# Attention and two expert layers on one core: the first expert prepared in border pools, output sums added in DRAM, scales from sums of squares, the seven products reordered

## Chip, core and metric

One NeuronCore of a Trainium2 chip runs the whole program in one launch. The metric is the time of one execution in microseconds (us), as the device measures it. The engines are PE (TensorE, the matrix unit), DVE (VectorE), ACT (ScalarE), POOL (GpSimd) and SP (SyncE, which issues DMAs); "the clock" is the TensorE clock granted, 1.00 being 2.4 GHz.

## What is computed

Three layers, cut to what matters:

```
x = attention(q, k, v, s)                       # 4 x 8 heads, 576 rows, 64 columns
x = gelu_like(x @ w_in) @ w_out                 # 2304 tokens, 512 -> 2048 -> 512
P = balance(softmax(x @ w_gate))                # 8 rounds over rows and columns
out = sum over e of P[:, e] * (relu(x @ w1[e]) @ w2[e])    # 8 experts, 512 -> 1024 -> 512
```

Every expert sees every token. The change touches the third layer and its beginning, which lies inside the end of the second.

## The kernel before

**Order of the work.** The kernel does not issue its instructions as it goes. Each one is handed to a planner, the class Sequencer, which keeps a time for every engine, gives each instruction a cost (`cost`) and a rank, and decides the order in which instructions go into each engine's queue. PE's steps come from generators that yield until their operands are ready by the planner's clock; held instructions of the other engines follow by readiness, rank and number. The result is a fixed list for each engine, which the chip works through in order: an instruction that waits holds up all behind it on its engine. All instructions carry the line of one helper (L260), so rows are told apart by tile names.

**Second layer's end.** `first_moe` ends with a wide stage: the last two token blocks go through `wide1` and `wide2` together, 16 steps, with dense PE work. Beside it, `begin_second` prepares the first third of the tokens for the experts (`prep_x(0)`), and half way through, when some weight buffers have become free, `begin_weights` prepares the first expert: `prep_w1(0, 0)`, `prep_w1(0, 1)`, then at lower priority `prep_w2(0)` and `prep_x(1)`.

**Third layer.** For each expert e and each third tp of the tokens (768 of them): four calls of `unit1` (j = 0 to 3; hidden columns) and then three calls of `unit2` (i = 0 to 2; output rows). That is 24 such thirds in all. Each unit is a matrix product in a Strassen-Winograd scheme with seven products instead of eight, every operand split into two f16 halves (three matmuls for each product and block of rows). A unit works in four PSUM banks A, B, C and D and chains its seven products through them: B starts as a copy of A, C as a copy of B. Two units are in flight at a time, in two sets of banks; PE takes the older one that is ready. Of `unit1`, a product is 6 matmuls of 384 columns; of `unit2`, 12 of 256.

In `unit1` the order of products is 0, 6, 5, 1, 4, 3, 2. The tile `hst` collects seven f32 pieces of hidden values, of which `parts` makes the f16 halves `h` in three groups of 3, 2 and 2 pieces: ACT writes the high half, DVE the low one. Product 3 goes into bank D on top of product 6, but DVE must first have read D for `hst[1]`, and that instruction also needs `v`, which ACT makes from bank C after product 4.

`unit2` needs the `h` of all four j, and begins with all 12 matmuls of product A(0, 0), then D(3, 6). Its seven products end in `acc2`, 18 tiles of 128 x 512 f32 that stay in SBUF through all experts: `put` adds to them with a DVE instruction each.

**Preparing an expert.** `weight_scales(e)` reads w1 and w2 of one expert (16 tiles `wm`), takes the largest absolute value on DVE and sends it through DRAM (`mx`, `row`) to all partitions. `prep_w1` and `prep_w2` load the weights again (`wr`), make the seven combinations and split them into halves (`w1o`, and `wo`, which goes to DRAM as `w2_d` and comes back as `w2o`). `prep_x` does the same for tokens (`xr`, `xo`, `xc_d` in DRAM, `xt` when loaded). `after1` sets them going: expert e + 1's scales at tp = 0, its w2 at tp = 1, its w1 at tp = 2.

Of the kernel before, what the change touches and what calls it, by code (L numbers as in the profile page):

```python
# [33 lines left out]
W2_ORDER = (0, 6, 5, 1, 4, 3, 2)  # L34
# [16 lines left out]
class Sequencer:  # L51
# [68 lines left out]
    def cost(self, engine, what, out, ins):  # L120
        n = max(self.size(x) for x in [out] + ins[:2])
        psum = any(x.space == PSUM for x in ins)
        if self.fine:
            if engine == "PE":
                return self.size(out) * (4 if ins[0].dtype == F32 else 1) / 2.4 + (13 if ins[0].dtype == F32R else 5)
            if engine == "DVE":
                quick = what in ("tensor_copy", "tensor_scalar") and not psum
                return 150 + n / (1.92 if quick else 0.96)
            if engine == "ACT":
                return 180 + n / 1.2  # L130
# [12 lines left out]


    def submit(self, engine, what, call, outs, ins):
# [5 lines left out]
        if what == "dma_start":  # L151
            op.cost = 60
            op.nbytes = self.size(outs[0]) * outs[0].shape[0] * 4
        else:
            op.cost = self.cost(engine, what, outs[0], ins)
# [146 lines left out]
def kernel(  # L302
# [45 lines left out]
    pa = ExitStack()  # L348
    wpool = Pool(seq, p1.enter_context(tc.tile_pool(name="wpool", bufs=1, side=left, reuse_waits="tile")))
# [783 lines left out]
    def scale_of(key, cols):  # L1133

        i = len(sc_of)
        sm = mem["small"]
# [21 lines left out]
        sc_of[key], inv_of[key] = s2[:, 0:1], s2[:, 1:2]  # L1158

    def raw(shape, name):  # L1160
        return mem["ep"].tile(shape, F32, tag="raw", name=name, bufs=7)

    def largest(col, x):
        nc.vector.tensor_reduce(out=col, in_=x, axis=AX.XY, op=ALU.max, apply_absolute_value=True)

    def weight_scales(e):

        mx = mem["small"].tile([128, 2, 8], F32, tag="wmx", name="wmx", bufs=2)
        for i in range(8):
# [5 lines left out]
            largest(mx[:, 0, i:i + 1], st)  # L1175
        scale_of(("w1", e), mx[:, 0])
        for i in range(8):
            st = raw([128, 1, DM], "wm")
            nc.sync.dma_start(out=st, in_=w2[e, i * 128:(i + 1) * 128, :].rearrange("p (o d) -> p o d", o=1))
            largest(mx[:, 1, i:i + 1], st)  # L1180
        scale_of(("w2", e), mx[:, 1])
# [111 lines left out]
    def prep_w2(e):  # L1293

        sc = sc_of["w2", e]
        for half in range(2):
# [10 lines left out]
            def part(i, src):  # L1307
                o = mem["ep"].tile([128, 2, 2, 256], F16, tag="xo", name="wo", bufs=2)
# [9 lines left out]

    xc_d = [dram.tile([128, 7, 2, 2, HT], F16, name=f"xc_d{tp}") for tp in range(NTP)]
# [62 lines left out]
    def cring(name):  # L1382
        return mem["c"].tile([128, HT], F32, tag="c", name=name, bufs=5)

    def unit1(e, tp, j, s):
# [28 lines left out]
        def parts(k0, k1, relu):  # L1414
            src = st[:, k0:k1]
# [17 lines left out]
        prod(d, 6)  # L1433
        yield ready(5, settled(b))
# [3 lines left out]
        u2, v, r21 = cring("u2"), cring("v"), cring("r21")  # L1438
        out_of(u2, b)
        yield ready(1, settled(a))  # L1440
        prod(a, 1, first=False)
        st = mem["st"].tile([128, 7, HT], F32, tag="hst", name="hst", bufs=2)
        seq.rank = 1
        out_of(st[:, 0], a, ACTF.Relu)
# [13 lines left out]
        if j == 0 and (e or tp):  # L1458
# [5 lines left out]
        parts(0, 3, True)  # L1464
        nc.vector.tensor_tensor(out=st[:, 3], in0=st[:, 0], in1=r21, op=ALU.subtract)
        nc.vector.scalar_tensor_tensor(
            out=st[:, 4], in0=st[:, 1], scalar=0.0, in1=r21, op0=ALU.max, op1=ALU.add
        )
        parts(3, 5, False)
        nc.vector.tensor_tensor(out=st[:, 5], in0=st[:, 4], in1=st[:, 0], op=ALU.subtract)  # L1470
        nc.vector.scalar_tensor_tensor(
            out=st[:, 6], in0=st[:, 2], scalar=0.0, in1=st[:, 5], op0=ALU.max, op1=ALU.subtract
        )
        parts(5, 7, False)
# [4 lines left out]
    def unit2(e, tp, i, s):  # L1479
# [7 lines left out]
        c11, c12 = acc2[t0][:, 0:256], acc2[t0][:, 256:512]  # L1487
        c21, c22 = acc2[t1][:, 0:256], acc2[t1][:, 256:512]
        ts = slice(i * 128, i * 128 + 128)

        def ready(k, n, *more):
            def when():
                t = max(ok(w[:, n]), *[m() for m in more])
                for j in range(NJ):
# [12 lines left out]
        def prod(o, k, n, first=True):  # L1507
            m = 0
            for j in range(NJ):
                for ph, pw in ((0, 0), (0, 1), (1, 0)):  # L1510
                    nc.tensor.matmul(
                        o, lhsT=hs[e, tp, j][:, ph, k, ts], rhs=w[:, n, pw, j],
                        start=(first and m == 0), stop=(m == 3 * NJ - 1), skip_group_check=not first,
                    )
                    m += 1

        def put(out, bank, t, first=True):
            if e == 0 and first:
                nc.scalar.activation(out=out, in_=bank, func=ACTF.Copy, scale=qs[0][:, tp:tp + 1])
            else:  # L1520
                by = pq[e][:, t:t + 1] if e else qs[0][:, tp:tp + 1]
                nc.vector.scalar_tensor_tensor(
                    out=out, in0=bank, scalar=by, in1=out, op0=ALU.mult, op1=ALU.add
                )

        def leave(t):
            if e == E - 1:
                nc.sync.dma_start(out=out[t * 128:(t + 1) * 128, :], in_=acc2[t])

        yield ready(0, 0, free("A"))  # L1530
        if e == 1:
            seq.rank = 1
            for t in (t0, t1):
                nc.vector.tensor_scalar(
                    out=acc2[t], in0=acc2[t], scalar1=prob[:, t, 0:1], scalar2=None, op0=ALU.mult
                )
            seq.rank = 0
        past[s] = False
        a = bank_tile("A", s)[:, 0:256]
        prod(a, 0, 0)  # L1540
        b = bank_tile("B", s)[:, 0:256]
        nc.scalar.copy(out=b, in_=a)
        yield ready(3, 6, free("D"))
        d = bank_tile("D", s)[:, 0:256]
        prod(d, 3, 6)
# [4 lines left out]
        yield ready(2, 1, settled(a))  # L1550
        prod(a, 2, 1, first=False)
        put(c11, a, t0)
        past[s] = True
        yield ready(4, 4, settled(c))
        prod(c, 4, 4, first=False)
        put(c22, c, t1)
        put(c22, d, t1, False)
        yield ready(1, 3, settled(d))
        prod(d, 1, 3, first=False)
        if e:  # L1560
            put(c21, d, t1)
            put(c21, b, t1)
        else:
            put(c21, b, t1)
            put(c21, d, t1, False)
        leave(t1)
        yield ready(6, 2, settled(c))
        prod(c, 6, 2, first=False)
        put(c12, c, t0)
        leave(t0)  # L1570
# [21 lines left out]
    def begin_second():  # L1592
# [4 lines left out]
        ))  # L1597
        mem["ps"] = Pool(seq, ctx.enter_context(
# [16 lines left out]
        )  # L1615
        seq.rank = 0

    def begin_weights():

# [3 lines left out]
        load_x2(0)  # L1623
        prep_w1(0, 0)
        prep_w1(0, 1)
        seq.rank = 3
        prep_w2(0)
        prep_x(1)
# [128 lines left out]
    wide2()  # L1757
    wpool.flush()
# [5 lines left out]
    for i in range(NTILE):  # L1764
        acc2[i] = xpool.tile([128, DM], F32, name=f"acc{i}")
# [99 lines left out]
    def after1(e, tp, j):  # L1865
# [6 lines left out]
        if tp == 0 and e + 1 < E:  # L1872
# [3 lines left out]
        if (e, tp) == (0, NTP - 1):  # L1876
# [113 lines left out]
```

## Time and profile before

| what | us |
|---|---|
| median of 3 runs (2237.88 to 2240.2) | 2238.88 |
| the profiled execution, its own time | 2241.58 |
| its span in the trace | 2239.7 |
| PE busy | 2001.8 (89%) |
| DVE busy | 1529.5 (68%) |
| ACT busy | 1099.3 (49%) |
| POOL busy | 364.1 (16%) |

PE is the engine with the most work, and matmuls overlap, so its busy time is not its least time; how far PE is from dense work is read from the distance between starts of equal groups. "Idle before" in a row is the time that the engine stood still before the group, with the instruction whose end released it.

### The profile page before, as it was taken

How to read it: one execution, taken by the hardware profiler on the slowest of the kernel's cores; microseconds unless marked ns; L12 is line 12 of the kernel's file. 1: busy time of each engine (PE TensorE's matmuls, PEld its weight loads, DVE VectorE, ACT ScalarE, POOL GpSimd, SP SyncE). 2: the span in 40 equal slices, each digit the busy share in tenths (PEclk: the TensorE clock that was granted, in tenths of full speed). 3: DMA queues.
4: the chain of work that ended last, by engine and by line, in shares of the span. 5: the costliest groups of instructions: out<-in, count | busy, mean ns of one | idle time of the engine just before them, and what ended most of it. 6: DMA issues, size and time to landing. Idle time of an engine off the chain costs nothing.

```text
span 2239.7 us, 40229 instructions
## 1 busy us (share of the span) xinstructions
PE 2001.8 (89%) x15782; PEld 1570.5 (70%) x15782; DVE 1529.5 (68%) x3120; ACT 1099.3 (49%) x2018; POOL 364.1 (16%) x376
## 2 busy tenths in 40 slices
PE   5889999999996598579999999999999999999998
PEld 3788999999874465446666666666666667766676
DVE  8886665545356265677786776778678778778555
ACT  6875655445335454444553453454455454345333
POOL 7774453443341210000000000000000000000000
PEclk9999999999998799789999999999999999999999
DMA  7454332221233534632343344335245234334220
GB/s 220 146 175 148 93 96 88 68 67 54 69 122 127 187 117 136 201 111 89 120 154 109 125 162 124 117 124 191 95 134 184 94 100 170 118 125 158 78 78 29
DMA packets 182897, 274.58 MB, mean 123 GB/s; under 512 B 17844, under 2 KB 132340, under 8 KB 182708
## 3 DMA queue, kind: packets, MB, share of 16 engines
q1 hardware_dynamic: 182708, 272.01, 37.0%
q8 instruction: 124, 2.03, 0.4%
q14 instruction: 65, 0.53, 0.1%
HBM read 219.77 MB, written 47.65 MB: 119 GB/s over the span
## 4 chain that ended last, share of the span: by engine, by line
PE 72%; DVE 18%; DMA 4%; ACT 3%; issue 2%; POOL 1%; SPq 0%; ACTq 0%; POOLq 0%; DVEq 0%
PE D L260 15%; PE C L260 15%; PE A L260 13%; PE B L260 8%; PE hp L260 7%; DVE h L260 6%; PE acc L260 5%; DVE hst L260 4%; PE sp L260 2%; PE tp L260 2%; PE op L260 2%; DVE t L260 2%; PE accw L260 2%; DMA wm<-in_moe_w_dram 1%; ACT h L260 1%
## 5 line engine op out<-in xcount | busy, mean ns | idle before, releaser
L260 PEld LDWEIGHTS <-h 128*128 128x128 f16 x6048 | 590.1, 99 | 176.0 <-DVE h L260 51.1
L260 PEld LDWEIGHTS <-w1o 128*128 128x128 f16 x4036 | 400.5, 100 | 384.4 <-issue 99.0
L260 ACT ACTIVATE h<-hst 128x768 f16<-128x768 f32 (+1 forms) x288 | 270.8, 948 | 140.6 <-DVE hst L260 136.9
L260 PE MATMUL D<-xt,w1o 128*128 128x384 f16 x1152 | 223.8, 335 | 84.9 <-DVE hst L260 47.7
L260 PE MATMUL A<-w2o,h 128*128 128x256 f16 x1728 | 223.1, 279 | 53.3 <-DVE h L260 25.5
L260 PE MATMUL A<-xt,w1o 128*128 128x384 f16 x1152 | 218.2, 330 | 23.0 <-DMA xt<-xc_d 22.3
L260 PE MATMUL D<-w2o,h 128*128 128x256 f16 x1728 | 211.5, 274 | 21.5 <-DVE h L260 12.9
L260 ACT COPY C<-B 128x384 f32<-128x384 f32 (+1 forms) x168 | 70.7, 421 | 312.0 <-PE B L260 311.3
L260 PE MATMUL C<-xt,w1o 128*128 128x384 f16 x1152 | 221.5, 332 | 0.2
L260 PE MATMUL C<-w2o,h 128*128 128x256 f16 x1728 | 209.1, 273 | 0.9 <-ACT C L260 0.2
L260 DVE TENSOR_TENSOR h<-hst,h 128x768 f16<-128x768 f32 x192 | 182.8, 956 | 11.3 <-ACT h L260 11.0
L260 ACT COPY B<-A 128x384 f32<-128x384 f32 (+1 forms) x168 | 70.2, 422 | 213.0 <-PE A L260 212.8
L260 PE MATMUL hp<-xh,wih 128*128 128x256 f32 (+1 forms) x512 | 155.2, 303 | 3.9 <-DVE t L260 3.9
L260 PE MATMUL hp<-xl,wih 128*128 128x256 f32 (+1 forms) x512 | 152.7, 298 | 0.0
L260 PE MATMUL hp<-xh,wil 128*128 128x256 f32 (+1 forms) x512 | 152.5, 298 | 0.0
L260 DVE SCALAR_TENSOR_TENSOR h<-hst,h 128x1152 f16<-128x1152 f32 x96 | 130.2, 1356 | 31.1 <-ACT h L260 30.4
L260 POOL TENSOR_TENSOR gl<-t,gh 128x512 fp32r<-128x512 f32 x72 | 95.8, 1330 | 171.3 <-ACT gh L260 120.0
L260 DVE SCALAR_TENSOR_TENSOR t<-t,hp 128x512 f32<-128x512 f32 x72 | 49.2, 683 | 106.5 <-ACT t L260 106.1
L260 DVE SCALAR_TENSOR_TENSOR acc<-D,pq,acc 128x256 f32<-128x256 f32 x126 | 60.9, 483 | 79.5 <-PE D L260 76.9
L260 ACT ACTIVATE sm<-sm,stats 64x576 f32<-64x576 f32 (+4 forms) x160 | 93.3, 602 | 43.3 <-DVE stats L260 42.5
L260 PE MATMUL B<-xt,w1o 128*128 128x384 f16 x576 | 113.2, 334 | 0.0
L260 PE MATMUL acc<-gh,woh 128*128 128x256 f32 x384 | 111.0, 289 | 0.0
(225 smaller groups left out, 3873.2 us busy)
## 6 DMA issues: line engine op xcount, KB each, us to landing
xt<-xc_d SPq DMA_DIRECT2D x168, 384.0 KB
wr<-in_moe_w_dram SPq DMA_DIRECT2D x128, 256.0 KB
w_d<-wo SPq DMA_DIRECT2D x112, 256.0 KB
w2o<-w_d SPq DMA_DIRECT2D x56, 512.0 KB
wm<-in_moe_w_dram SPq DMA_DIRECT2D x112, 256.0 KB
kq<-in_qk_dram SPq DMA_DIRECT2D x32, 448.0 KB
kq<-in_qk_dram SPq DMA_DIRECT2D x32, 256.0 KB
st<-in_moe_w_in_dram SPq DMA_DIRECT2D x16, 512.0 KB
```

The costliest lines, as they stand in the source:

```text
L260: self.seq.submit(self.name, what, lambda: method(*args, **named), outs, ins)
```

## The change

In words. (1) The tiles `raw` and `wo` come from a pool that can be changed: `prep_w2(0)` and `prep_x(1)` move into `begin_second`, with a border pool `bp1` of their own, and `begin_weights` closes that pool, opens a second one (`bp2`, 12 buffers), prepares w1 there, and then runs `weight_scales(1)`, which `after1` no longer does at e = 0. (2) `acc2` is gone. Each `unit2` writes its two row blocks into tiles `y` (4 buffers); `put` scales on DVE or ACT, whichever the planner finds less loaded, and `more` adds on DVE. Expert 0 writes `y` to DRAM (`y0_d`); expert 1 loads that back (`yb`), adds and writes `acc_d`; experts 2 to 6 add into `acc_d` by an accumulating DMA that POOL issues; expert 7 loads `acc_d`, adds and writes the output. (3) The scales come from sums of squares, which ACT makes while it reads the tile, in place of DVE's largest value. (4) `unit1` runs its products in the order 0, 6, 5, 3, 4, 1, 2: ACT copies bank D out right behind product 6 (`m7`), and `parts` works in four groups, of 1, 2, 2 and 2 pieces. `unit2` runs products A and D for the first three j, then the rest of A, then D or A(2, 1), and the others. (5) `balance` is started by the last gate instead of by the last `unit1` of expert 0, and the planner's costs of scaled instructions and of POOL's DMAs are higher.

```diff
+    def squares(col, x):
+        nc.scalar.activation(out=x, in_=x, func=ACTF.Square, scale=SHRINK, accum_out=col)
...
-            largest(mx[:, 0, i:i + 1], st)
+            squares(mx[:, 0, i:i + 1], st)
...
@@ unit1
+        u2, m7 = cring("u2"), cring("m7")
+        out_of(m7, d)
         yield ready(5, settled(b))
         prod(b, 5, first=False)
...
         out_of(u2, b)
+        yield ready(3, settled(d))
+        prod(d, 3, first=False)
+        st = mem["st"].tile([128, 4, HT], F32, tag="hst", name="hst", bufs=3)
+        r11, c22, c21, r21 = (st[:, k] for k in range(4))
+        join(c21, d, u2)
+        yield ready(4, settled(c))
+        prod(c, 4, first=False)
+        join(c22, c, m7)
         yield ready(1, settled(a))
         prod(a, 1, first=False)
...
-        yield ready(4, settled(c))
-        prod(c, 4, first=False)
-        out_of(v, c)
-        join(st[:, 1], d, v)
-        yield ready(3, settled(d))
-        prod(d, 3, first=False)
-        join(st[:, 2], d, u2)
...
-        parts(0, 3, True)
+        parts(0, 1, st[:, 0:1], True)
+        parts(1, 3, st[:, 1:3], True)
...
@@ unit2
+        def put(out, bank, t):
+            by = pq[e][:, t:t + 1] if e else qs[0][:, tp:tp + 1]
+            if seq.load("DVE") < seq.load("ACT"):
+                nc.vector.tensor_scalar(out=out, in0=bank, scalar1=by, scalar2=None, op0=ALU.mult)
             else:
+                nc.scalar.activation(out=out, in_=bank, func=ACTF.Copy, scale=by)
...
+        def leave(t, y):
...
+            if e in (1, E - 1):
+                before[t] = mem["st"].tile([128, DM], F32, tag="yb", name="yb", bufs=2)
+                nc.sync.dma_start(out=before[t], in_=(y0_d if e == 1 else acc_d)[t])
+            if e == 0:
+                nc.sync.dma_start(out=y0_d[t], in_=y)
...
+            elif e < E - 1:
+                nc.gpsimd.dma_start(out=acc_d[t], in_=y, accum_op=ALU.add)
...
+        yield ready(0, 0, free("A"), part=most)
+        prod(a, 0, 0, part=most)
+        yield ready(3, 6, free("D"), part=most)
+        prod(d, 3, 6, part=most)
+        yield ready(0, 0, part=last)
+        prod(a, 0, 0, part=last)
...
@@ begin_second, begin_weights
+        mem["raw"], mem["wo"] = (bp, 7), (bp, 2)
+        prep_w2(0)
+        mem["raw"], mem["wo"] = (mem["ep"], 7), (mem["ep"], 2)
+        prep_x(1)
...
+        end_border()
...
+        mem["raw"], mem["bp"] = (bp, 12), bp
         prep_w1(0, 0)
         prep_w1(0, 1)
         seq.rank = 3
-        prep_w2(0)
-        prep_x(1)
+        weight_scales(1)
```

What the planner makes of it, at three places (`wm` are weights read for scales, `w_d` is `w2_d`, `x_d` is `x2_d`, `m` is `m7`).

SP's queue around the first load of `w2o`, which `unit2` of expert 0 needs. Before:

```order
L260 DMA w_d_2_139<-wo 256x1x512
L260 DMA w_d_0_137<-wo 256x1x512
L260 DMA xr<-x_d_67 128x384
L260 DMA w2o<-w_d_0_137 128x2048
L260 DMA w_d_6_143<-wo 256x1x512
L260 DMA w_d_5_142<-wo 256x1x512
L260 DMA xr<-x_d_67 128x384
L260 DMA w2o<-w_d_6_143 128x2048
```

And now:

```order
L261 DMA xr<-x_d_67 128x384
L261 DMA x_d_68<-xo 128x512 x4
L261 DMA w2o<-w_d_0_137 128x2048
L261 DMA w2o<-w_d_1_138 128x2048
L261 DMA w2o<-w_d_6_143 128x2048
L261 DMA w2o<-w_d_5_142 128x2048
L261 DMA w2o<-w_d_4_141 128x2048
L261 DMA w2o<-w_d_3_140 128x2048
L261 DMA w2o<-w_d_2_139 128x2048
```

The stores of `w_d` that stood between the loads are all ahead of the wide stage's last stores (`x_d_68`), so the seven loads stand together.

ACT's queue at the end of the wide stage. Before:

```order
L260 ACTIVATE t<-hp 128x512
L260 ACTIVATE w1o<-ws,early 128x512
L260 ACTIVATE w1o<-wr,early 128x512
L260 ACTIVATE xo<-accw 128x512 x4
L260 ACTIVATE w1o<-wr,early 128x512
L260 ACTIVATE lt<-gp,ig 128x48
L260 COPY B_9590<-A_9583 128x384
```

And now:

```order
L261 ACTIVATE t<-hp 128x512
L261 ACTIVATE wm,wmx<-wm 128x512 x9
L261 ACTIVATE xo<-accw 128x512 x4
L261 ACTIVATE xr<-xr,early 128x384
L261 CAST xo_8832<-xr 128x384
L261 CAST xo_8833<-xt_8830 128x384
L261 ACTIVATE lt<-gp,ig 128x48
L261 COPY B_9772<-A_9765 128x384
```

Nine squares of the next expert's weights now stand between the last tanh and the copies that empty the wide stage's banks and that the first `unit1` waits for.

ACT's queue in the last `unit1` of a third, in the middle of the third layer. Before:

```order
L260 COPY C_18715<-B_18696 128x384
L260 ACTIVATE u_18716<-B_18696 128x384
L260 ACTIVATE h<-hst 128x768
L260 ACTIVATE h<-hst 128x1152
L260 ACTIVATE h<-hst 128x768
L260 ACTIVATE r_18647<-C_18644 128x384
L260 ACTIVATE v<-C_18715 128x384
L260 ACTIVATE hst<-A_18689 128x384
```

And now:

```order
L261 ACTIVATE m_19127<-D_19119 128x384
L261 COPY C_19137<-B_19103 128x384
L261 ACTIVATE u_19126<-B_19103 128x384
L261 ACTIVATE h<-sb 128x768
L261 ACTIVATE h<-sa 128x768
L261 ACTIVATE hst<-A_19096 128x384
L261 ACTIVATE wo<-wr,sc_18538 128x512
L261 ACTIVATE h<-hst 128x384
L261 ACTIVATE h<-hst 128x768
```

The instruction that frees bank D for product 3 was DVE's sum with `v`, four ACT instructions behind the copy to C; now it is `m`, ahead of that copy.

## Rows read from the trace of the kernel before

**Rows 1.** Stretches: us, busy (count) of PE, PEld, DVE, ACT, POOL; clock, DMA share, GB/s.

```profile
583.00:676.00 93.00, 89.81 (x384) 72.25 (x383) 46.49 (x68) 34.83 (x63) 42.26 (x32) 0.97 0.36 119
706.50:989.90 283.40, 191.16 (x1399) 133.24 (x1399) 159.84 (x313) 130.02 (x245) 26.01 (x24) 0.83 0.44 145
989.90:2202.20 1212.30, 1125.71 (x8400) 821.14 (x8400) 899.99 (x1576) 567.20 (x1009) 0.00 (x0) 0.99 0.38 126
1599.00:1780.00 181.00, 168.26 (x1260) 122.83 (x1260) 137.96 (x242) 86.66 (x154) 0.00 (x0) 0.99 0.40 134
```

**Rows 2.** PE's timeline, end of one third: start, us, group, count, idle before it and releaser.

```profile
1781.14 1.14 PE L260 MATMUL D<-xt,w1o 128*128 128x384 f16 x6 [2.19 <-DVE hst L260]
1782.11 1.14 PE L260 MATMUL C<-xt,w1o 128*128 128x384 f16 x6
1783.09 1.49 PE L260 MATMUL A<-w2o,h 128*128 128x256 f16 x11
1785.58 1.59 PE L260 MATMUL A<-w2o,h 128*128 128x256 f16 x13 [1.00 <-DVE h L260]
1787.01 1.64 PE L260 MATMUL D<-w2o,h 128*128 128x256 f16 x11
1789.44 1.59 PE L260 MATMUL D<-w2o,h 128*128 128x256 f16 x13 [0.79 <-DVE h L260]
1790.87 1.47 PE L260 MATMUL B<-w2o,h 128*128 128x256 f16 x12
1792.17 1.47 PE L260 MATMUL A<-w2o,h 128*128 128x256 f16 x12
```

**Rows 3.** PE's timeline, experts 0 and 1: the long waits.

```profile
723.38 5.20 PE L260 MATMUL A<-w2o,h 128*128 128x256 f16 x24 [14.79 <-DMA w2o<-w_d]
...
737.37 4.13 PE L260 MATMUL A<-w2o,h 128*128 128x256 f16 x24 [3.55 <-DMA w2o<-w_d]
...
780.59 2.08 PE L260 MATMUL A<-xt,w1o 128*128 128x384 f16 x6 [20.51 <-DMA xt<-xc_d]
...
947.17 0.82 PE L260 MATMUL D<-xt,w1o 128*128 128x384 f16 x2 [23.40 <-ACT w1o L260]
...
974.06 0.82 PE L260 MATMUL D<-xt,w1o 128*128 128x384 f16 x2 [8.19 <-ACT w1o L260]
```

**Rows 4.** Groups by form: busy us, mean ns of one, idle before, releasers.

```profile
L260 DVE TENSOR_REDUCE wmx<-wm 128x1 f32<-128x512 f32 x112 | 71.3, 675 | 8.4 <-DMA wm<-in_moe_w_dram 8.3
L260 DVE SCALAR_TENSOR_TENSOR acc<-D,pq,acc 128x256 f32<-128x256 f32 x126 | 60.9, 483 | 79.5 <-PE D L260 76.9
L260 ACT ACTIVATE w1o<-wr,sc 128x512 f16<-128x512 f32 x70 | 49.5, 719 | 9.4 <-DMA wr<-in_moe_w_dram 4.9 <-DVE wr L260 4.6
L260 ACT ACTIVATE v<-C 128x384 f32<-128x384 f32 x96 | 46.8, 487 | 16.7 <-PE C L260 15.1
L260 ACT ACTIVATE acc<-C,qs 128x256 f32<-128x256 f32 x18 | 8.5, 474 | 26.7 <-PE C L260 26.7
L260 DVE TENSOR_TENSOR h<-hst,h 128x768 f16<-128x768 f32 x192 | 182.8, 956 | 11.3 <-ACT h L260 11.0
L260 ACT ACTIVATE h<-hst 128x768 f16<-128x768 f32 x192 | 161.1, 842 | 100.7 <-DVE hst L260 100.1
```

**Rows 5.** Stretches of 5 us with the most DMA traffic, columns as in rows 1.

```profile
640.00:645.00 5.00, 5.00 (x24) 4.14 (x23) 4.74 (x4) 2.66 (x5) 4.37 (x3) 1.00 1.02 388
...
935.00:940.00 5.00, 0.00 (x0) 0.00 (x0) 2.17 (x3) 2.14 (x4) 0.00 (x0) 0.50 1.01 355
```

**Rows 6.** SP's DMA queue: issues of `xt` and of the scales' `mx` and `row`.

```profile
776.42 3.96 SPq L260 DMA_DIRECT2D xt<-xc_d  x7
...
851.64 1.28 SPq L260 DMA_DIRECT2D mx<-m  x2
...
862.27 0.80 SPq L260 DMA_DIRECT2D row<-mx  x2
```

More of the change, by code (lines that the diff above doesn't have):

```diff
@@ L151, in submit @@
         if what == "dma_start":
-            op.cost = 60
-            op.nbytes = self.size(outs[0]) * outs[0].shape[0] * 4
+            op.cost = 60 if engine == "SP" else 1000
+            op.nbytes = self.size(outs[0]) * outs[0].shape[0] * (2 if self.fine and outs[0].dtype == F16 else 4)
         else:
@@ L1317, in load_w2 @@
             nc.sync.dma_start(out=w2s[e][:, i], in_=w2_d[e % 2][i])
+    y0_d = [dram.tile([128, DM], F32, name=f"y0_d{t}") for t in range(NTILE)]
+    acc_d = [dram.tile([128, DM], F32, name=f"acc_d{t}") for t in range(NTILE)]
     xc_d = [dram.tile([128, 7, 2, 2, HT], F16, name=f"xc_d{tp}") for tp in range(NTP)]
@@ L1505, in free, with prod @@
             return lambda: bank_free(role, s)
[L1507 to L1510, printed above, removed]
+        def prod(o, k, n, first=True, part=range(NJ)):
+            for j in part:
+                for m, (ph, pw) in enumerate(((0, 0), (0, 1), (1, 0))):
                     nc.tensor.matmul(
                         o, lhsT=hs[e, tp, j][:, ph, k, ts], rhs=w[:, n, pw, j],
-                        start=(first and m == 0), stop=(m == 3 * NJ - 1), skip_group_check=not first,
+                        start=(first and j + m == 0), stop=(j == NJ - 1 and m == 2), skip_group_check=not first,
@@ new lines, in more @@
+        def more(out, bank, t):
+            by = pq[e][:, t:t + 1] if e else qs[0][:, tp:tp + 1]
+            nc.vector.scalar_tensor_tensor(out=out, in0=bank, scalar=by, in1=out, op0=ALU.mult, op1=ALU.add)
+        def leave(t, y):
+            seq.rank = 1
+            if e in (1, E - 1):
[3 more added lines that the diff above has]
+                nc.sync.dma_start(out=y0_d[t], in_=y)
+            elif e == 1:
@@ L1522, in put @@
                 nc.vector.scalar_tensor_tensor(
-                    out=out, in0=bank, scalar=by, in1=out, op0=ALU.mult, op1=ALU.add
+                    out=y, in0=before[t], scalar=prob[:, t, 0:1], in1=y, op0=ALU.mult, op1=ALU.add
                 )
[L1526 to L1536, printed above, removed]
+                nc.sync.dma_start(out=acc_d[t], in_=y)
+            elif e < E - 1:
+                nc.gpsimd.dma_start(out=acc_d[t], in_=y, accum_op=ALU.add)
+            else:
+                nc.vector.tensor_tensor(out=y, in0=before[t], in1=y, op=ALU.add)
+                nc.sync.dma_start(out=out[t * 128:(t + 1) * 128, :], in_=y)
@@ L1542, in unit2 @@
         nc.scalar.copy(out=b, in_=a)
-        yield ready(3, 6, free("D"))
-        d = bank_tile("D", s)[:, 0:256]
-        prod(d, 3, 6)
+        y0, y1 = (mem["st"].tile([128, DM], F32, tag="y", name="y", bufs=4) for _ in range(2))
+        whole_d = ready(3, 6, part=last)
+        done_d = whole_d() <= seq.free["PE"]
+        if done_d:
+            prod(d, 3, 6, part=last)
+            put(y1[:, 256:512], d, t1)
+        yield ready(2, 1, settled(a))
+        prod(a, 2, 1, first=False)
+        put(y0[:, 0:256], a, t0)
@@ L1546, in unit2 @@
+        past[s] = True
+        if not done_d:
+            yield whole_d
+            prod(d, 3, 6, part=last)
+            put(y1[:, 256:512], d, t1)
         yield ready(5, 5, settled(b))
@@ L1549, in unit2 @@
         nc.scalar.copy(out=c, in_=b)
[L1550 to L1553, printed above, removed]
+        nc.scalar.activation(
+            out=y1[:, 0:256], in_=b, func=ACTF.Copy, scale=pq[e][:, t1:t1 + 1] if e else qs[0][:, tp:tp + 1]
+        )
         yield ready(4, 4, settled(c))
         prod(c, 4, 4, first=False)
-        put(c22, c, t1)
-        put(c22, d, t1, False)
+        more(y1[:, 256:512], c, t1)
         yield ready(1, 3, settled(d))
         prod(d, 1, 3, first=False)
[L1560 to L1566, printed above, removed]
+        more(y1[:, 0:256], d, t1)
+        leave(t1, y1)
         yield ready(6, 2, settled(c))
         prod(c, 6, 2, first=False)
-        put(c12, c, t0)
-        leave(t0)
+        put(y0[:, 256:512], c, t0)
+        leave(t0, y0)
         done2[0] += 1
@@ L1623, in begin_weights @@
         load_x2(0)
+        bp = Pool(seq, border.enter_context(
+            tc.tile_pool(name="bp2", bufs=1, side=left, reuse_waits="tile")
+        ))
+        mem["raw"], mem["bp"] = (bp, 12), bp
         prep_w1(0, 0)
@@ L1763 @@
     mem["h"] = mem["c"] = mem["st"] = mem["w2"] = xpool
-    for i in range(NTILE):
-        acc2[i] = xpool.tile([128, DM], F32, name=f"acc{i}")
+    mem["wo"] = xpool, 3
     ep = mem["small"]
```

100 lines of the change are left out of this document (61 added, 39 removed).

## The prediction

> **What bounds the kernel now.** I read the stretches first, then PE's timeline, then the groups. A third of the tokens (four `unit1`, three `unit2`) needs 28 products of 0.975 us and 21 of 1.30 us; these are the distances between starts of equal groups in dense work [rows 2]. That makes 27.3 + 27.3 = 54.6 us, below which this PE stream cannot go. The 20 thirds between 989.9 and 2202.2 took 60.6 us each [rows 1], so 6.0 us of each is not dense work. Where they go stands in [rows 2]: product 3 of the last `unit1` waits 2.19 us for DVE's `hst`, and from 1783.09 to 1790.87 PE spends 7.78 us on four products that take 5.2, since the halves `h` of the last j are late. Together 4.8; the rest is shorter waits and matmuls at a lower clock behind them. DVE is busy 138.0 of 181.0 us and ACT 86.7 [rows 1], so it is the order of a chain, not an engine's sum, that PE waits for.
>
> The other loss is the border. Between 706.5 and 989.9 lie three thirds, 163.8 us if dense, in 283.4 [rows 1]: 119.6 us too many. Five waits hold 14.79 + 3.55 (for `w2o`) + 20.51 (for `xt`) + 23.40 + 8.19 (for `w1o`) = 70.4 of them [rows 3]; three thirds of ordinary loss hold 18; the remaining 31 are the gates, `balance` and matmuls at a lower granted clock, of which this stretch has 0.83 on average [rows 1].
>
> **Product order in unit1.** The chain that held product 3 was bank C's product 4, `v` (0.487 us on ACT [rows 4]), DVE's sum, PE. Now one ACT instruction of that size reads D straight behind product 6, and product 5 (0.975 us) runs meanwhile. It is late only if an `h` of 0.842 us [rows 4] is in ACT's way: 0 to 0.84 us. I take 0.2, since the planner puts it ahead of the copy to C.
>
> **Order in unit2.** Two `unit2` begin together. Work that doesn't need the last j's late pieces is now 9 matmuls of A and 9 of D in each, the last 3 of A, A(2, 1), and the last 3 of D: 72 of 0.108 us or 7.8 us. The first product that needs a late piece, B, started in the trace without a wait 7.78 us after `unit1` was through [rows 2]. One group of A (0.98 us) is placed ahead of `unit1`'s end, so 0 to 1.0 us is left. I take 0.5. With 1.1 for what I can't see (DVE and ACT still work in a fixed order) 1.8 us stay of the 6.0: a gain of 4.2 a third, between 2 and 5.4. Twenty thirds give **84 us**.
>
> **Border.** The first `w2o` waited for stores of `w_d` made late; now those stores are ahead of the wide stage's end. Seven loads of 0.52 MB (128 x 2048 in f16) at 355 GB/s [rows 5] take 10.3 us, and a first load takes 4.2 from issue to use (776.42 in [rows 6] to 780.59 in [rows 3]); both fit under the four `unit1`, 27.3 us. `xt` for the second third needs 7 loads of 0.39 MB, 7.8 + 4.2 us under three `unit2`, its source being finished before. `w1o` of expert 1 waited for scales that were begun at tp = 0; now they are begun before the third layer, and its two halves are prepared beside 40 us of PE work, as in later thirds, which show no such wait. The price is more work in the wide stage and just behind it. ACT gets 9 squares between the last tanh and the first copies; the nearest row is `w1o`, the same shape, 0.719 us [rows 4], so 6.5 us, less what lies under the last 5.4 us of PE work; behind stand four `xo`. I leave 20 us of the border's loss standing: 6 for this queue, 5 for expert 1's `w1o`, 9 for gates, `balance` and clock. So 119.6 - 18 - 20 = 81.6, and three thirds at 4.2, 12.6: **94 us**.
>
> **Sums of squares.** 112 reductions of 0.675 us leave DVE [rows 4] and 112 squares of about 0.72 come to ACT. Neither is on PE's path by its sum: an expert's ACT work becomes 86.7 + 16 x 0.72 + 31 scaled outputs at 0.474 + 2 for the extra `h` group = 115 us, DVE's 138.0 - 16 x 0.675 - 36 x 0.483 + 5 x 0.48 = 112 us, both of some 169 us. At nothing, then; the cover is PE's stream, and if ACT ran late the price is that of the third rival.
>
> **Output sums.** No DMA that POOL issues, and none that adds, is in the trace. Its nearest rows are a load's 4.2 us, and 10.6 us from the issue of `mx`, a tiny store behind seven `xt` loads, to the `row` that waits for it [rows 6]. What counts is when the buffer is needed again: of four `y`, the third `unit2` writes the first's, after 24 + 12 + 12 + 9 + 9 + 3 + 3 = 72 matmuls, 7.8 us later. So the wait is 0 to 2.8 us, once a third in experts 2 to 6: 0 to 42 us in all. I take 0, as the add is nearer to a single load than to a queue of seven. In experts 1 and 7 DVE waits for a load `yb` that SP issues; 0 to 4.2 us in six thirds, I take 1 each: **minus 6**. At the very end the added DVE sum costs 1 us, and the last third's own end gains 4: plus 3.
>
> **Sum.** 84 + 94 - 6 + 3 = 175 us from 2241.6, the profiled execution's own time (its span is 1.9 less), gives 2066.6; the median of the runs lies 2.7 lower: **2064 us**.
>
> **Rivals.**
> *Border limited by DMA.* The wide stage moved 119 GB/s for 93 us [rows 1], 11.1 MB. Added are, by the tiles' shapes, 5.8 MB for w2 (8 loads, 14 stores), 5.1 for x (12 and 14) and 4.2 for `wm` (16 loads): 26.2 MB, or 281 GB/s. The traffic reached 388 and 355 in single stretches of 5 us [rows 5], so it fits, but nowhere for long. At 200 GB/s it takes 131 us; the first `unit1` starts 38 us late, behind squares that wait for their tiles, and cold: 2064 + 42 = 2106.
>
> *The adds hold the outputs up.* If POOL's DMA takes L from issue to landing, ACT or DVE stands still for L - 7.8 us before the third `unit2`'s first output, with the next `unit1`'s copies queued behind: 15 thirds. The gain is gone at L = 7.8 + 175 / 15 = 19.5 us; at 25 it costs 258 us: 2322, slower. How it could come: POOL's own work on the DMA is held up by DVE's instructions, which fill three quarters of the time [rows 1] in pieces of up to 0.956 us [rows 4]; twelve of those over the wait of 7.8 would do it. Against: the slowest landing seen is 10.6 us. The Trainium skill, page "SBUF — State Buffer", section "A bandwidth-pool intuition that's wrong (but worth ruling out)", speaks against this change: descriptors of a DMA issued from GpSimd are generated on its cores, which a DVE instruction using both ports locks out, so that a DMA of about 620 ns took about 3100 beside a DVE copy. By that page's 2.5 us on top, an estimate, L would be 6.7 to 13.1 us and the loss 0 to 80; no row of this trace shows it.
>
> *ACT becomes the bound.* In four `unit1` ACT now has about 5.9 us of work a unit (six instructions of 0.487, three of 0.842, one of 0.49) in 6.8 of PE's; squares and preparation must find the rest. If they delay each unit by 1 us, 92 units lose 92: 2156. For it: the orders are fixed, and one late instruction holds up all behind it. Against: by its sum ACT is free for a third of the time.
>
> *It doesn't do what it says.* The waits of [rows 3] move to the next late thing (`w1o`, the last third's tokens), and the ends of the thirds stay: within 0.2% of before. Against: the orders show the stores gone from between the loads, and `m` ahead.
>
> **Numbers.** The forecast, 2030 to 2110: 0.70; better than 2030: 0.04; DMA-limited border: 0.11; ACT: 0.06; adds: 0.06, of which 0.05 slower than before; no change: 0.03, of which I give 0.02 to "within" and 0.01 to slower. A measurement can tell some 0.2% from no change. So faster by over 0.2%: 0.92; within: 0.02; slower: 0.06. The range reaches from 2030 (0.9 us left a third and 12 in the border: 102 + 105 - 6 + 3 = 204 of gain) to 2150 (half of the thirds' gain, 42, with 50 in the border: 89 of gain), and takes in the bound of 42 us for the adds on top of the forecast; it leaves 0.19 out.
>
> **What would show it.** Right: thirds of 55.5 to 57 us from expert 1 on; no wait on `hst` ahead of D and less than 1 us on `h`; between the first and the fourth third's ends about 190 us in place of 283; no wait for `w2o`, `xt` or `w1o` over 5 us; granted clock 0.95 and more there; DVE some 150 us less busy, ACT some 180 more. Wrong: idle time of ACT or DVE released by a DMA `acc_d<-y`; PE idle ahead of the first `unit1` for over 10 us; PE waiting for ACT's copies between units; thirds of 59 us and more.

## The result, and the profile after

| | median us | runs | lowest to highest |
|---|---|---|---|
| before | 2239.54 | 4 | 2237.88 to 2243.42 |
| changed | 2100.45 | 4 | 2094.25 to 2106.07 |

The changed kernel takes 0.938 of the time before (95% interval 0.9345 to 0.9407): 139 us less. The profiled execution is the fastest of its four, 2094.25 us with a span of 2092.5. Sums by engine, from its page:

```profile
PE 1970.6 (94%) x15782; PEld 1565.2 (75%) x15782; DVE 1407.9 (67%) x2927; ACT 1250.8 (60%) x2540; POOL 457.5 (22%) x473
```

The stretches that answer to [rows 1], with the same columns: the wide stage, three thirds between the last `unit1` of the first third and that of the fourth, the twenty thirds after them, and three thirds out of these.

```profile
583.00:690.00 107.00, 92.86 (x404) 73.07 (x403) 75.08 (x93) 56.11 (x115) 65.86 (x47) 0.97 0.69 217
724.70:920.70 196.00, 177.14 (x1393) 129.00 (x1392) 139.19 (x300) 111.73 (x222) 17.16 (x15) 0.96 0.46 156
920.70:2060.80 1140.10, 1106.37 (x8407) 820.64 (x8405) 773.27 (x1373) 712.29 (x1487) 77.91 (x90) 1.00 0.62 166
1547.50:1719.60 172.10, 166.10 (x1262) 123.00 (x1261) 116.02 (x209) 109.44 (x229) 15.59 (x18) 1.00 0.66 169
```

The bounds of [rows 1] lie at the start of product 3 of those last `unit1`, the bounds above at their end. Measured in both traces at the start of the last matmul of `unit1`, the spans of 2239.7 and 2092.5 divide like this:

| stretch | before | after | gain | forecast |
|---|---|---|---|---|
| to the last `unit1` of the first third | 708.3 | 724.5 | -16.2 | inside the border's 94 |
| three thirds at the border | 283.4 | 195.9 | 87.5 | 94 |
| twenty thirds | 1212.3 | 1139.6 | 72.7 | 84, less 6 |
| behind them | 35.7 | 32.5 | 3.2 | 3 |
| sum | | | 147.2 | 175 |

A third now takes 57.0 us in place of 60.6. The end of one, to be held against [rows 2] (PE's timeline):

```profile
1775.53 1.14 PE L261 MATMUL C<-xt,w1o 128*128 128x384 f16 x6
1776.50 1.15 PE L261 MATMUL A<-w2o,h 128*128 128x256 f16 x9
1777.48 2.13 PE L261 MATMUL D<-w2o,h 128*128 128x256 f16 x18
1779.45 0.82 PE L261 MATMUL A<-w2o,h 128*128 128x256 f16 x6
1780.50 2.78 PE L261 MATMUL A<-w2o,h 128*128 128x256 f16 x24 [0.23 <-ACT B L261]
1783.12 0.82 PE L261 MATMUL D<-w2o,h 128*128 128x256 f16 x6
1783.77 1.36 PE L261 MATMUL B<-w2o,h 128*128 128x256 f16 x11
1785.91 1.59 PE L261 MATMUL B<-w2o,h 128*128 128x256 f16 x13 [0.78 <-DVE h L261]
```

The wait for `hst` is gone, and groups of 9 matmuls that need only three of the four `h` stand where PE used to wait. One wait for `h` is left, 0.78 us ahead of B. At the border, the three longest waits, which answer to [rows 3]:

```profile
690.65 0.38 PE L261 MATMUL B<-w1o 128*128 128x512 f16 x1 [2.92 <-ACT xo L261]
...
904.47 0.82 PE L261 MATMUL D<-xt,w1o 128*128 128x384 f16 x2 [8.20 <-ACT w1o L261]
...
945.38 1.36 PE L261 MATMUL A<-w2o,h 128*128 128x256 f16 x11 [3.08 <-ACT B L261]
```

No wait for `w2o` or `xt` is among them. The groups new since [rows 4] (by form): a square is two instructions, and POOL spends 0.88 us on each adding DMA.

```profile
L261 ACT ACTIVATE wm<-wm 128x512 f32<-128x512 f32 x112 | 69.2, 621 | 32.2 <-DMA wm<-in_moe_w_dram 32.1
L261 ACT ACTIVATION_READ_ACCUMULATOR wm<-wm 128x1 f32 x112 | 21.3, 190 | 0.0
L261 POOL DMA_DIRECT2D acc_d<-y x90 | 77.9, 884 | 1050.9 <-DVE y L261 961.8 <-ACT y L261 49.4 <-DVE wr L261 39.5
```

### The profile page after: what moved, and what is told of

It is laid out like the page before. It is cut to its first block, busy times and chain, and to the rows that moved or that the text cites. A ratio compares the mean times of both kernels' runs of the same rounds, so it can differ in the third digit from the quotient of the medians.

```text
span 2092.5 us, 41023 instructions
## 1 busy us (share of the span) xinstructions
PE 1970.6 (94%) x15782; PEld 1565.2 (75%) x15782; DVE 1407.9 (67%) x2927; ACT 1250.8 (60%) x2540; POOL 457.5 (22%) x473
## 4 chain that ended last, share of the span: by engine, by line
PE 50%; issue 24%; DVE 11%; DMA 7%; POOL 4%; ACT 3%; SPq 1%; POOLq 0%; ACTq 0%; DVEq 0%
PE C L261 9%; PE D L261 8%; PE A L261 7%; PE hp L261 7%; PE acc L261 6%; PE B L261 4%; DVE h L261 2%; PE sp L261 2%; POOL acc_d L261 2%; PE tp L261 2%; PE op L261 2%; DVE t L261 2%; DMA w_d<-wo 1%; DMA wm<-in_moe_w_dram 1%; DMA xc_d<-xo 1%
## 5 line engine op out<-in xcount | busy, mean ns | idle before, releaser
L261 PEld LDWEIGHTS <-w1o 128*128 128x128 f16 x4036 | 395.5, 98 | 270.8 <-issue 12.1
L261 POOL DMA_DIRECT2D acc_d<-y x90 | 77.9, 884 | 1050.9 <-DVE y L261 961.8
L261 PE MATMUL D<-xt,w1o 128*128 128x384 f16 x1152 | 218.9, 328 | 10.2 <-ACT w1o L261 8.2
L261 PE MATMUL A<-w2o,h 128*128 128x256 f16 x1728 | 216.2, 272 | 10.4 <-ACT B L261 10.4
L261 PE MATMUL C<-w2o,h 128*128 128x256 f16 x1728 | 210.1, 274 | 15.5 <-ACT C L261 12.2
L261 PE MATMUL D<-w2o,h 128*128 128x256 f16 x1728 | 220.7, 273 | 0.5 <-DVE h L261 0.5
L261 DVE SCALAR_TENSOR_TENSOR h<-hst,h 128x768 f16<-128x768 f32 (+1 forms) x192 | 144.3, 760 | 45.0 <-ACT h L261 42.9
L261 ACT ACTIVATE h<-hst 128x768 f16<-128x768 f32 (+1 forms) x192 | 128.8, 678 | 6.7 <-DVE hst L261 6.7
L261 PE MATMUL B<-w2o,h 128*128 128x256 f16 x864 | 107.8, 275 | 15.6 <-DVE h L261 9.6
L261 ACT ACTIVATE hst<-A 128x384 f32<-128x384 f32 x96 | 47.0, 489 | 121.2 <-PE A L261 120.4
L261 ACT ACTIVATE t<-hp 128x512 f32<-128x512 f32 x72 | 42.8, 594 | 112.5 <-PE hp L261 111.3
```

The lines of the kernel that those rows point to most:

```text
L261: self.seq.submit(self.name, what, lambda: method(*args, **named), outs, ins)
```

## Experiments

All twelve are the changed kernel with one or a few edits; "against it" is the difference of medians. Each edit makes the planner order everything anew, and the changed kernel's own runs lie 12 us apart, so differences of a few us say nothing. Two parts of the change were not undone by any run: the output sums in DRAM as a whole (2), and the earlier start of `balance` with the planner's other prices (5). What these are worth is not shown.

| | median us | ratio to before, 95% | against it |
|---|---|---|---|
| 1 old unit1 order | 2102.19 | 0.9373 to 0.9407 | +2 |
| 2 old unit2 beginning | 2115.74 | 0.9436 to 0.9467 | +15 |
| 5 both old | 2147.40 | 0.9554 to 0.9630 | +47 |
| 4 largest values on DVE | 2072.25 | 0.9245 to 0.9277 | -28 |
| 6 square's price | 2086.22 | 0.9292 to 0.9341 | -14 |
| 10 price and later loads | 2084.29 | 0.9288 to 0.9313 | -16 |
| 8 six `y` | 2088.89 | 0.9312 to 0.9355 | -12 |
| 11 largest and six `y` | 2070.29 | 0.9228 to 0.9252 | -30 |
| 3 border undone | 2130.46 | 0.9504 to 0.9548 | +30 |
| 7 sums on DVE | 2101.49 | 0.9361 to 0.9404 | +1 |
| 9 and three `wo` | 2085.84 | 0.9274 to 0.9324 | -15 |
| 12 together | 2061.34 | 0.9190 to 0.9216 | -39 |

**The orders of the products (1, 2, 5).** My theory was that each order takes its own wait away.

```diff
 # 1: unit1 again 0, 6, 5, 1, 4, 3, 2
-        out_of(m7, d)
...
+        out_of(v, c)
+        join(c22, d, v)
 # 2: unit2
-        prod(a, 0, 0, part=most)
...
+        prod(a, 0, 0)
...
+        prod(d, 3, 6)
```

> The changed kernel (2100 us) with unit1's products in the old order again (0, 6, 5, 1, 4, 3, 2; v from bank C, no copy of D behind product 6). My theory: the new order took a wait of about 2 us for hst ahead of product 3 out of each third, so 24 thirds give it back: 2140 to 2150 us, with that wait back in the trace at 1.5 to 2.2 us. Rival: the thirds became shorter through unit2's order and a less loaded DVE alone: 2095 to 2110 us.

> The changed kernel (2100 us) with unit2's beginning in the old order (all 12 matmuls of product A, then all 12 of D). My theory: work that needs no late piece lasts 2.1 us longer a third in the new order, and 24 thirds give that back: 2140 to 2155 us, with waits for h of 0.8 to 2 us ahead of A and D of the first unit2. Rival: with the halves h in four groups and earlier, the order of unit2 no longer matters: 2095 to 2110 us.

Nearly nothing, the rival's time; and 15 us, between theory and rival. So I took both back at once:

> The changed kernel (2100 us) with both old orders, unit1's products and unit2's beginning. Each alone cost 2 and 15 us. Theory one: the two orders stand in for each other, each hides the same lateness, and without both the thirds go back to 60 us: 2150 to 2175 us, with the waits for hst and h of the kernel before. Theory two: what shortened the thirds is mostly the outputs' sums taken off DVE and out of the chain (DVE 581 us busy in experts 2 to 6 against 689 before) and the planner's prices, the orders add up and are worth little: 2112 to 2125 us.

Experts 2 to 6 (15 thirds), by stretch, of the changed kernel and of run 5, each from the end of expert 1's last third to that of expert 6's:

```profile
1065.86:1923.92 858.06, 830.54 (x6309) 615.62 (x6306) 581.36 (x1042) 548.38 (x1147) 76.61 (x89) 1.00 0.66 169
```

```profile
1066.86:1970.00 903.14, 842.23 (x6296) 618.21 (x6294) 579.32 (x1042) 559.24 (x1145) 76.52 (x89) 0.98 0.60 161
```

A third is 57.2 us in the one and 60.2 in the other; before it was 60.8 there. DVE is as little busy in both. So of 3.6 us gained a third in these experts the orders bring 3.0, and the sums taken off DVE with all the rest about 0.6, in which the loss by the squares (1.0, run 4 below) is contained. Of the 45.1 us between the two stretches, 33.6 are longer waits of PE (for `hst` 25.3 in place of none, for `h` 14.5 in place of 8.8, for ACT's copies into C 20.8 in place of 9.9) and 11.7 are PE's own busy time, at a granted clock of 0.98 in place of 1.00. But the orders are no two gains: the waits for `hst` ahead of D, in the whole program, are these in the kernel before, in run 1 and in run 5 (what PE waited for: us in total, times, longest):

```profile
PE D L260 <- DVE hst L260: 47.7, 25, 4.2
```

```profile
PE D L261 <- DVE hst L261: 18.0, 24, 1.3
```

```profile
PE D L261 <- DVE hst L261: 36.4, 23, 2.1
PE C L261 <- ACT C L261: 23.6, 12, 5.0
PE D L261 <- DVE h L261: 21.3, 25, 1.9
```

With unit2's new beginning PE has nine matmuls ready that it does while `hst` is late, and `hst` costs 0.75 us; with unit1's new order the `h` are early enough that unit2's beginning matters less. Theory one of run 5 holds, though a little less than it expected comes back: experts 0 and 1 change by 2 us together, expert 7 by 7.5.

The medians of single runs mix this with the border. Between the profiled executions run 1 is 8 us slower, not 2. In experts 2 to 6, clear of the border, run 1 and run 2 take

```profile
1062.68:1928.26 865.58, 831.66 (x6302) 613.69 (x6300) 577.41 (x1042) 560.53 (x1145) 76.80 (x89) 1.00 0.63 168
```

```profile
1071.32:1942.53 871.21, 836.87 (x6301) 615.03 (x6300) 575.94 (x1038) 555.98 (x1149) 76.72 (x89) 0.99 0.64 167
```

which is 7.5 and 13.2 us more than the changed kernel. Unit1's new order is thus worth something by itself; but without both 45.1 us are lost, over twice the sum.

**The scales (4, 6, 10).**

```diff
 # 4
-            squares(mx[:, 0, i:i + 1], st)
+            largest(mx[:, 0, i:i + 1], st)
 # 6
-            op.cost = self.cost(engine, what, outs[0], ins)
+            op.cost = self.cost(engine, what, outs[0], ins) + 190 * (self.fine and len(outs) > 1)
 # 10: 6, and around the loads of wm
+            seq.late = 4000.0
```

> The changed kernel (2100 us) with the scales from DVE's largest absolute value again, no squares on ACT. My theory: neither engine's sum is on PE's path, so 2094 to 2107 us, ACT some 90 us less busy and DVE some 75 more. Rival one: the squares hold ACT up in the thirds (57.2 us in experts 2 to 6 against 54.7 in expert 7, which prepares nothing): the third in which they run becomes 1 us shorter or more and the wide stage's end loses its queue of nine: 2075 to 2092. Rival two: DVE's queue becomes what PE waits for: 2110 to 2130.

28 us faster, rival one and 3 us beyond its range: the squares are the dearest part of the change. What PE waited for in experts 2 to 6, changed kernel first:

```profile
PE C L261 <- ACT C L261: 9.9, 9, 2.3
PE B L261 <- DVE h L261: 6.9, 10, 0.8
PE A L261 <- ACT B L261: 5.0, 12, 0.8
PE C L261 <- DVE y L261: 3.3, 4, 1.2
PE B L261 <- ACT h L261: 1.9, 5, 0.4
```

```profile
PE C L261 <- ACT C L261: 5.6, 8, 1.1
PE A L261 <- ACT B L261: 4.9, 15, 0.4
PE C L261 <- DVE y L261: 2.7, 5, 1.0
```

27.0 and 13.2 us in sum: ACT's copies and the `h` that begin on ACT are what was late. In these experts ACT is 548 us busy with squares and 513 without, DVE 581 and 615. Of 25 us between the two profiled executions 15 lie in experts 2 to 6 (858.1 and 842.9 us), 7 in experts 0 and 1, and 4 ahead of the first `unit1`. Two reasons were possible, a false plan or the load:

> The changed kernel (2100 us), in which only the planner's price of a square is raised by 190 ns, to what the trace shows (619 ns and 189 ns for reading the accumulator, priced at 627). Theory one: the squares cost 28 us because the planner packs ACT's queue with 3 us an expert that do not exist, and the fixed order is late by that: 2075 to 2090 us. Theory two: the load itself costs, squares on ACT that wait for their tiles in front of the copies PE needs (25 us of ACT's waits for wm in experts 2 to 6), whatever the price: 2094 to 2107 us.

> The changed kernel (2100 us) in which the planner's price of a square is 190 ns higher, and a load of wm is taken to land 4 us later than the planner had it. The price alone gave 14 of the 28 us. Theory one: the squares cost what they do because the planner has them ready too early, so that ACT stands in front of a load (25.9 us in experts 2 to 6) with PE's copies behind; with later loads these waits fall below 10 us and the rest of the 28 comes back: 2070 to 2080 us. Theory two: what is left is ACT's work itself, 15 us more in each expert than with DVE's largest value: 2083 to 2092 us.

The price alone gives 14 us back, inside theory one's range, but half of the 28. Later loads take ACT's waits for `wm` in experts 2 to 6 from 25.4 to 9.8 us, and the time stays at 2084. So half of the 28 went with a price that knew nothing of the accumulator's 0.19 us, and the waits for tiles were not the other half. The stretches tell the halves apart. Experts 2 to 6 in run 4, then in run 6:

```profile
1054.86:1897.78 842.92, 829.11 (x6301) 615.65 (x6300) 614.71 (x1087) 512.63 (x1010) 76.59 (x89) 1.00 0.65 172
```

```profile
1054.96:1910.98 856.02, 830.63 (x6302) 613.54 (x6301) 577.99 (x1042) 551.20 (x1145) 76.57 (x89) 1.00 0.63 170
```

There the price gives back 2 us of the 15, and with later loads (run 10) it is 3. What it gives back lies in experts 0 and 1 (8 us) and ahead of them (3), as much as run 4 gains there. So theory one, a queue packed too tightly, fits the border alone; in the thirds behind it ACT's extra work itself is what is left, and no run shows which order would hide it.

**The output sums (8, 11).**

```diff
-tag="y", name="y", bufs=4)
+tag="y", name="y", bufs=6)
```

> The changed kernel (2100 us) with six buffers y in place of four. Theory one: the wait of ACT for the adding DMA to free a y (14.2 us in experts 2 to 6, up to 4.1 us at a time) reaches PE as waits of 1.0 to 2.35 us for copies into C and for y; without it 5 to 10 us less: 2090 to 2096 us, and no wait of ACT or DVE on a DMA from y. Theory two: those waits lie beside other work, and PE's waits for C have another cause: 2097 to 2104 us.

Theory one, 1 us beyond its range. Between the profiled executions it is 5 us and not 12, 4 of them in experts 2 to 6, where the ring works. In the changed kernel, the adding DMAs from issue to landing (the view of the tile `acc_d`):

```profile
DMA to landing us min/median/max: 4.0/5.6/12.2
```

And one place, on ACT's timeline and then on PE's:

```profile
1803.58 0.47 ACT L261 ACTIVATE y<-A,pq 128x256 f32<-128x256 f32 x1 [4.06 <-DMA acc_d<-y]
1803.95 0.38 ACT L261 COPY C<-B 128x256 f32<-128x256 f32 x1
```

```profile
1804.38 1.47 PE L261 MATMUL C<-w2o,h 128*128 128x256 f16 x12 [1.82 <-ACT C L261]
```

ACT stands 4.06 us for a `y` whose add has not landed; the copy into C is queued behind, and PE waits 1.82. With six buffers ACT waits for no such DMA, though the landings are as before (3.7, 5.8, 12.2).

> The changed kernel (2100 us) with both edits that helped: largest values on DVE instead of squares (2072) and six buffers y (2089). Theory one: the two losses lie in different waits (copies behind squares; a y held by an adding DMA) and add up: 2058 to 2066 us. Theory two: both act on ACT's lateness before the copy into C, so the second gives little more: 2067 to 2074 us.

Theory two: with the squares gone too, the ring is worth 2 us. ACT then has time to come back from such a wait before PE needs it: in run 4 it stands longer for the adds than in the changed kernel, where this was 14.7 us, and yet PE waits less for its copies into C (5.6 us in experts 2 to 6, not 9.9).

```profile
ACT y L261 <- DMA acc_d<-y: 23.3, 10, 4.0
```

The two losses are one lateness with two causes.

**The border (3, 7, 9).**

```diff
 # 3
-        prep_w2(0)
...
-        prep_x(1)
...
-        weight_scales(1)
+        prep_w2(0)
+        prep_x(1)
...
-        if tp == 0 and 0 < e < E - 1:
+        if tp == 0 and e < E - 1:
```

> The changed kernel (2100 us) with the border as before: w2 of expert 0 and the second third's tokens prepared behind w1, the scales of expert 1 begun at tp = 0. My theory: the earlier preparation is what took the waits for w2o, xt and w1o away; the border's gain in the trace was 56 + 28 - 14 = 70 us, nearly all of which goes: 2160 to 2175 us, waits of 10 to 25 us back, and the wide stage 14 us shorter. Rival: half of the border's gain comes from the orders of the units and balance's earlier start, and the earlier preparation only moves waits: 2110 to 2135 us.

30 us, so the rival. In the profiled executions experts 0 and 1 take 46 us more, and the first `unit1` starts at 682.1 in place of 691.1. What PE waits for in experts 0 and 1 (stretch from 680 to 1120 us):

```profile
PE A L261 <- DMA xt<-xc_d: 15.3, 1, 15.3
PE D L261 <- ACT w1o L261: 14.1, 1, 14.1
PE D L261 <- DVE w1o L261: 10.6, 2, 9.6
PE D L261 <- DMA xt<-xc_d: 4.3, 2, 3.5
```

`xt` and `w1o` are back, but not `w2o`, 18.3 us in [rows 3], although w2 is again prepared behind w1. Something else in the change removed that wait: the first load of `w2o` is issued at 692.90 us here and at 719.67 in the kernel before. The second border pool, whose 12 buffers stay in use here, is the likely cause, and that was not tried. In all the three thirds at the border take 237 us in run 3, 283 before and 196 in the changed kernel: more than half of their gain does not need the early preparation.

The other side of the border is the wide stage, 14 us longer than before. Run 7 takes the sums of expert 0's weights off POOL:

```diff
 # 7
-        both = nc.vector.tensor_tensor if e else of_two
+        both = nc.vector.tensor_tensor
 # 9: 7, and
-        mem["raw"], mem["wo"] = (bp, 7), (bp, 2)
+        mem["raw"], mem["wo"] = (bp, 7), (bp, 3)
```

> The changed kernel (2100 us) with the sums of expert 0's weights all on DVE, none on POOL. Theory one: POOL's 16 sums of 1.5 to 1.7 us hold gl up, for which PE waits 8.5 us in the wide stage, and DVE's instructions beside them take twice their time (w1o 0.75 to 1.73 us): the first unit1 starts at 678 to 686 us in place of 691, total 2086 to 2096 us. Theory two: the wide stage is bound by its loads and stores (DMA share 0.92 between 640 and 660 us), so the first unit1 stays at 690 or comes later by DVE's longer queue: 2098 to 2110 us.

Neither earlier nor later: theory two's numbers. PE's waits for POOL's `gl` fall from 8.5 to 3.3 us in the stage, but one new wait of 10.77 takes their place. ACT's timeline, and PE's:

```profile
631.68 0.72 ACT L261 ACTIVATE wo<-wr,early 128x512 f16<-128x512 f32 x1 [3.34 <-DMA w_d<-wo]
636.38 0.72 ACT L261 ACTIVATE wo<-wt,early 128x512 f16<-128x512 f32 x1 [3.97 <-DMA w_d<-wo]
640.46 0.72 ACT L261 ACTIVATE wo<-wr,early 128x512 f16<-128x512 f32 x1 [3.37 <-DMA w_d<-wo]
```

```profile
642.63 0.80 PE L261 MATMUL accw<-gl,woh 128*128 128x512 f32 x1 [10.77 <-DVE gl L261]
```

When the first border pool is closed, `flush` issues what is left of `prep_w2(0)` at once. With two buffers `wo` each further half waits for a store, on ACT, then on DVE, and `gl` stands behind them. One buffer more:

> The changed kernel (2100 us) with expert 0's sums on DVE, as in the run before, and three buffers wo in the first border pool in place of two. In that run one wait of PE for gl lasted 10.8 us: where the first border pool is closed, three pairs of wo stood in ACT's and DVE's queues ahead of gl, each waiting 3.3 to 4.0 us for a store of the pair before. Theory one: this chain of stores is what ate the gain of taking the sums off POOL; with a third buffer that wait falls below 6 us and the first unit1 starts at 680 to 687 us: 2090 to 2097 us. Theory two: the wide stage is bound by the volume of its loads and stores, and the wait moves on to a load: first unit1 at 690 or later, 2098 to 2106 us.

Theory one, and 4 us better than its range, though the six runs lie as far apart as 2069 and 2091: that wait is gone, and the first `unit1` starts 12 us earlier, 1.5 us later than in the kernel before, with all the new preparation ahead of it (timeline, then the stage's stretch):

```profile
678.79 1.45 PE L261 MATMUL A<-xt,w1o 128*128 128x384 f16 x6
```

```profile
583.00:678.00 95.00, 89.96 (x408) 71.78 (x407) 76.18 (x114) 56.33 (x117) 36.45 (x28) 1.00 0.76 241
```

The loads were there all along and did not bound it: 241 GB/s over the stage in place of 217.

**Together (12).**

> The changed kernel (2100 us) with largest values on DVE, six buffers y, expert 0's sums on DVE and three buffers wo in the first border pool. Theory one: the wide stage's loss (12 us, first unit1 at 678.8 in place of 691.1) and the squares' loss lie in different places and add up: 2053 to 2064 us, first unit1 at 675 to 682 us. Theory two: with the largest values too, DVE has too much in the wide stage and its gain goes: 2066 to 2075 us, first unit1 at 685 us or later.

Theory one: 2061.34 us (2060.51 to 2062.37 in five runs), 39 less than the changed kernel and the fastest here. The first `unit1` starts at 677.7, and in the wide stage DMA carries more than I thought it would have to:

```profile
640.00:660.00 20.00, 17.30 (x74) 13.43 (x73) 20.00 (x22) 10.50 (x19) 13.09 (x9) 1.00 0.91 297
```

## Why the prediction was right, and where it was wrong

The direction and the range held: 2100 us in 2030 to 2150, 36 above the forecast of 2064. (The 204 us of gain behind the range's lower end give 2035, not 2030.) Some 28 of the 36 are gain that didn't come (147 of 175 us); the other 9 are the runs' spread, since I put the median 2.7 below the profiled execution and it lies 6.2 above.

**Where the 28 are.** By the stretches 23 of them lie at the border (71 us came, 87.5 less 16.2, in place of 94) and 5 in the twenty thirds (72.7 in place of 78). That the thirds came so near is in part luck: without the squares (run 4, one profiled execution) the twenty thirds take 14 us less, so all else gains 87 there where 78 was forecast, and that hid 9 of the 14. At the border run 4 gives back 11 us of the 23, and run 9, with the squares in place, 11 ahead of the last `unit1` of the first third.

**What would show it right.** Thirds of 55.5 to 57: 57.0, on the edge. No `hst` wait ahead of D, less than 1 us on `h`: so, apart from expert 0. First to fourth third 190 us: 196. No wait for `w2o`, `xt`, `w1o` over 5 us: one of 8.20 for `w1o`. Clock 0.95: 0.96. DVE 150 less, ACT 180 more: 122 and 152. Of the signs for "wrong", two came, both small: ACT idle behind a DMA `acc_d<-y` (14 us in experts 2 to 6), and PE waiting there for ACT's copies into B and C (15 us).

**Squares of nothing: the step that failed most.** I set the two engines' sums, 115 and 112 us an expert, against 169 and called PE's stream the cover. Run 4 showed 28 us. A sum says that an engine can do its work, not that it does it before PE asks. I had that mechanism as the third rival, at 1 us a unit and 2156 us; it came true at a third of that size. Nor had I priced a square as two instructions, 0.81 us by the trace and not 0.72.

**The ring of `y` at 0.** The bounds were 0 to 42 us and I took the lower end, since an add looked nearer to a single load (4.2) than to 10.6. Run 8 measured 12 by the medians, 5 between the profiled executions. The median landing of 5.6 fits my reading, below the 7.8 us of slack; the longest, 12.2, make the wait. The price was in the tail, not in the middle. The other term of the outputs, 6 us for the loads of `yb`, does not show in expert 7: DVE waits 5.3 us for them, and yet a third takes 54.7 us, the dense 54.6. The estimate drawn from the Trainium skill's page "SBUF — State Buffer", section "A bandwidth-pool intuition that's wrong (but worth ruling out)", 6.7 to 13.1 us, lies above the median and takes in the longest; no run shows that DVE's instructions caused it.

**4.2 us a third from two orders.** I added 2.0 and 2.1 as if each order had its own wait. Undone singly they cost 2 and 15 us, both together 47, or 2.0 a third over 24; in experts 2 to 6 it was 7.5, 13.2 and 45.1. The chains were read rightly; that one order's spare work also covers the other's wait was missed.

**94 us at the border, 6 for the queue at the wide stage's end.** The three thirds gained 87.5, near enough, but not for my reason alone: undoing the early preparation costs 30 us, and the wait for `w2o` stays away without it. The price, put at 6, was 16 us ahead of the last `unit1` of the first third, and the nine squares were the smaller part of it: run 4, without them, takes 4 back, and run 9, with them, 11, by moving sums off POOL and giving `wo` a buffer.

**The rivals.** "Border limited by DMA" gave 2106, close to the result, and is still false: the first `unit1` was 14 us late and not 38, and runs 9 and 12 move the same data with none of that delay. A number that fits proves no mechanism. The adds held outputs up by 5 to 12 us, far from the 258 that this rival gave for a landing of 25 us; "it doesn't do what it says" fell with the first look at the waits.

## What to carry to other kernels

Work moved to an engine with time to spare is free only if its place in that engine's fixed order is: look at what is queued behind it and who waits for that, and price each instruction as the trace has it, second instruction included. Gains that act on the same wait don't add, so undo each alone and both together before crediting either, and compare by stretch as well as by total. Where a ring is freed by a DMA and something urgent is queued behind the wait, size it by the longest landing, not by the median.

## What the runs showed of the hardware

**An adding DMA is usable as an accumulator.** 256 KB issued by POOL land in 4.0 to 12.2 us, median 5.6, for 0.88 us of POOL's time, beside a DVE that is busy two thirds of the time.

**DVE and POOL slow each other.** In the changed kernel's wide stage one `w1o` takes DVE 0.75 us alone and up to 1.7 beside sums on POOL, and one sum takes POOL 1.28 us alone and 1.74 beside them (DVE's timeline, then POOL's; DVE's second row holds two instructions):

```profile
647.03 0.75 DVE L261 SCALAR_TENSOR_TENSOR w1o<-wr,early,w1o 128x512 f16<-128x512 f32 x1 [1.04 <-ACT w1o L261]
...
657.20 3.47 DVE L261 SCALAR_TENSOR_TENSOR w1o<-wr,early,w1o 128x512 f16<-128x512 f32 x2
```

```profile
598.21 1.28 POOL L261 TENSOR_TENSOR wr<-wr 128x512 f32<-128x512 f32 x1
...
656.69 1.74 POOL L261 TENSOR_TENSOR wr<-wr 128x512 f32<-128x512 f32 x1
658.39 1.74 POOL L261 TENSOR_TENSOR wr<-wr,ws 128x512 f32<-128x512 f32 x1
```

With the sums on DVE its busy time in the stage hardly grows, 75.1 to 76.2 us, while POOL's falls from 65.9 to 36.5. The Trainium skill, page "SBUF — State Buffer", section "SBUF: two separate sides", says that a GpSimd operation that reads SBUF and a DVE one with two SBUF inputs lock each other out of a shared pair of ports, whichever starts first holding it for a whole instruction. The trace agrees in that both grow longer, from 0.75 and 1.28 us to 1.7 each; that whole instructions take turns it does not show.
